# Nine transposed-sum matmuls in one run, sixteen placing loads split over two queues, and a longer wait for host positions

## The chip, the core and the metric

The kernel runs on one core of a Trainium2 chip. The metric is the device time of one execution in microseconds (us). Matrix products run on TensorE (PE), element-wise work on VectorE (DVE) and ScalarE (ACT), and GpSimd (POOL) and SyncE (SP) mainly issue DMA loads and stores; each engine works off its own queue in order.

## The reference

Both halves start from the same normalised input `xn = layernorm(x)`, with 2048 tokens and 576 channels. The result is `x + s * silu(mlp(xn))`.

```
xn = _layernorm(x, axis=-1)
P  = exp((A * dt[:, None])[:, :, None] * pos)
K  = 2.0 * einsum("dn,dnl->dl", C, P).real
y  = irfft(rfft(xn.T, 2L) * rfft(K, 2L))[:L]
s  = y + xn * D_skip
h  = gelu(einsum("bsd,df->bsf", layernorm(xn), w1) + b1)
g  = silu(einsum("bsf,fd->bsd", h, w2) + b2)
out = x + s * g
```

So there is an MLP with 4608 hidden units, and beside it a long convolution per channel whose 2048 taps K come from 128 complex exponentials.

## The kernel before, in words

**The MLP sets the frame.** Hidden units are handled in groups of 384 (three tiles of 128), tokens in blocks of 512. One pair of group and block is a *slot*; there are 48, numbered from 0. A slot has 11 positions: three tiles of layer 1 (line L546, 14 matmuls of 512 columns each, since every fp32 operand is split into a high and a low part), and then eight pieces of layer 2. ACT makes the hidden tile (gelu, L578, then its high part hh, L581) and DVE the low part hl (L584).

Layer 2 in most slots (44 of 48) has two kinds of matmul. *Plain* ones (L638) hold 128 tokens of the hidden tile and stream 448 columns of w2; a key from 0 to 3 names which 128 tokens of the block. The other 128 output channels are computed *turned* (T, L630): w2 is held, 512 tokens are streamed, and the sum lands transposed in a PSUM bank that stays in use over many slots. A slot has nine turned matmuls. The table PLAN (L1296) gives the order of the pieces: a pair like `("T", both)` means the turned matmuls of hidden tiles 0 and 1 (six), `(0, both)` the plain ones of key 0 for the same two tiles (six).

**Four times the turned sums are brought back**, at slots 18, 22, 44 and 45 (CONV). DVE adds the bias (`total_rest`, L651) and transposes 32 by 32 blocks into the tile `bias2` (`turn_rest`, L655). `place_rest` (L657) then moves the blocks to their places in the accumulator with 16 loads from SBUF to SBUF, all from the SP queue (L663).

**The convolution rides between.** Its matmul groups stand as *guests* between pieces of a slot: K is the making of taps from tables (`kgen`, L981, 36 of them), F the first transform (L1053), S the second with the product (L1092), I the inverse (L1145), O the last stage (L1177). A K group may stand alone, or *ride*: go directly in front of another guest, its host (`ride`, L992). The tables for K come from DVE and ACT work on parameters that `load_par` (L876) loads on the POOL queue (L881): a phase product (L899, L902), rounding on ACT (L905), and so on. Chunk results go to DRAM by eight stores on the POOL queue (L1188: four from tile pr, four from tile ys).

**The order of all this is planned while the program is written**, by a small model of the engines (class `Order`): each step has an engine, a duration, a due time, and what it needs. The model's verdict is the order on every engine. `pe_turns` (L1538) lets guests in after certain positions; a K that could stand alone is held back until it has been ready for ALONE us. Loads that are issued inside another step's function, and steps with no engine (such as `load_par`, 4.5 us), take no queue time in the model.

Of the kernel before, what the change touches and what calls it, by code (L numbers as in the profile page):

```python
# [18 lines left out]
P = 128  # L19
# [16 lines left out]
G = 3  # L36
# [3 lines left out]
DA = 448  # L40
# [3 lines left out]
def dve(n):  # L44
    return 0.075 + 0.00104 * n
# [163 lines left out]
def step(eng, dur, fn, need=(), mark=None, cv=0, at=0.0, late=0.0, tbl=None, by=1e9):  # L209
    return dict(eng=eng, dur=dur, fn=fn, need=tuple(need), mark=mark, cv=cv, at=at, late=late, tbl=tbl, by=by)  # L210
# [3 lines left out]
def mixer_kernel(ctx, tc, u, log_a_real, a_imag, c_real, c_imag, log_dt, d_skip, w1, b1, w2, b2,  # L214
                 f1, f2, g2, g1, tvals, ident, out, parts=("mlp", "s4d")):
    nc = tc.nc
# [17 lines left out]
    def dram(ap_of, offset, ap):  # L234
        return bass.AP(tensor=ap_of.tensor, offset=ap_of.offset + offset, ap=ap)
# [30 lines left out]
    bias2 = sb.tile([P, D], F32, name="bias2")  # L266
# [387 lines left out]

        nc.vector.transpose(bias2[:, :TB].rearrange("p (j d) -> p j d", j=4), rest(tb))  # L655

    def place_rest(tb):  # L657

        o = rest(tb)
        x = bias2[:, :TB].rearrange("p (j v d) -> p j v d", j=4, v=4)  # L660
        for c in range(4):
            for v in range(4):
                nc.sync.dma_start(o[32 * v:32 * v + 32, :, 32 * c:32 * c + 32], x[32 * c:32 * c + 32, :, v])  # L663
        if tb == 1:
            nc.sync.dma_start(bias2[:, :DA], dram(b2, 0, [[0, P], [1, DA]]))

    def tanh_half(z):
        t = sb.tile([P, TB], F32, name="h32", bufs=2)[:, :288]
# [541 lines left out]
    NPOS = G + 8  # L1210
    NSLOT = 4 * NG
    od = Order(tc, nc)
# [80 lines left out]
    MA, MT = 0.2034, 0.2303  # L1293
    CONV = {2 * NG - 6: 0, 2 * NG - 2: 1, 4 * NG - 4: 0, 4 * NG - 3: 1}
    both, allof = (0, 1), (0, 1, 2)
    PLAN = [("T", both), (0, both), ("T", (2,)), (0, (2,)), (1, allof), (2, allof), (3, (0,)), (3, (1, 2))]  # L1296
    ENDS = {True: {2: 0, 3: 1, 5: 2, 7: 3}, False: {3: 0, 4: 1, 5: 2, 7: 3}}

    def lens(slot):
# [134 lines left out]
    def weigh_in(which):  # L1434

        m = KB + 1 if which == 1 else G
        ln = lens(turn[0] - 1)
        end = od.t["PE"] + sum(ln[G:] if which == 1 else ln[:G])
        apart = which == 2 and SEQ[turn[0]][0] not in JOINED
        for i in range(m):  # L1440
            by = end - ((2.2, 1.5, 0.4)[i] if apart else 0.8 * (m - i))
            cell = []
            n = (DA, G * DT, 2 * DA)[i] if apart else G * P if which == 1 else D
            k = len(WM)
            WM.append(which)
            wl["steps"].append(step("ACT", act(n), lambda c=cell: c.append(split_raw()), need=[("raw", k + (apart and i == 1))],
                                    mark=("wh", k), by=by - 0.9, at=od.t["PE"] + od.LAT))

            def low(c=cell, k=k, n=n):
                k0 = state["load"]  # L1450
                c[0]()
                for j in range(k0, state["load"]):
                    od.marks["raw", j] = od.t["DVE"] + dve(n) + 5.5 + 1.0 * (j - k0)
            wl2["steps"].append(step("DVE", dve(n), low, need=[("wh", k)], mark=("w", k), by=by))

    WM = [1] * (KB + 1)
# [35 lines left out]
    part = {}  # L1492
# [40 lines left out]

    pace = dict(left=NCH * (2 + 2 + 4), last=0.0, started=False)
    END = 930.0
    ALONE = 5.0

    def pe_turns(limit=1, any_time=False, all_lines=True):  # L1538
        for x in (nl, pl, ml) + ((c3, c1, kl) if all_lines else ()):
            n = 0  # L1540
            while n < (2 if x in (c1, nl) else limit):
                h = od.head(x)
                if h is None or h[0]["eng"] != "PE" or h[1] > od.t["PE"] + (0.3 if x is nl else -0.40):
                    break
                if x is c1:
                    now = od.t["PE"]
                    gap = (END - now) / max(pace["left"], 1)
                    if n == 0 and pace["started"] and now < pace["last"] + 0.50 * gap and not any_time:
                        break
                    pace["started"], pace["last"] = True, now  # L1550
                    pace["left"] -= 1
                if x is kl and pace["started"] and kl["steps"][0]["mark"][1] < NB - 1 and od.t["PE"] < h[1] + ALONE:
                    break
                behind = ride(h[0]) if x in (c1, c3) else None
                od.run(x)
                if behind:
                    behind()
                od.pin()
                od.advance(od.t["PE"])
                n += 1  # L1560
# [64 lines left out]
    for slot in range(NSLOT):  # L1625
        turn[0] = slot + 1
        n, g, tb = SEQ[slot]
        change = slot + 1 < NSLOT and SEQ[slot + 1][0] != n
        final = slot >= NSLOT - 2
        for pos in range(NPOS):  # L1630
# [28 lines left out]
            else:  # L1659
                turned = slot in TURNED  # L1660
                if turned:
                    j, terms, last, hid = l2_terms(pos - G)
# [18 lines left out]
                if j == "T" and slot in CONV and 2 in terms:  # L1681
                    od.urgent.append((od.t["PE"], [step("DVE", dve(TB), lambda tb=tb: total_rest(tb), by=od.t["PE"] + 4.0),
                                                   step("DVE", dve(TB), lambda tb=tb: turn_rest(tb), by=od.t["PE"] + 6.0),
                                                   step("SP", 1.0, lambda tb=tb: place_rest(tb), mark=("placed", slot))]))
                look_ahead(pos)
                if last or halves:
                    add = cell[0]
# [26 lines left out]
            for f in LATER.get((slot, pos), ()):  # L1714
                f()
            od.advance(od.t["PE"])
            pe_turns(all_lines=pos in (0, 1, G + 1, G + 3, G + 5, NPOS - 1))
    od.force(lambda: not od.urgent and not any(x["steps"] for x in od.lines))


# [52 lines left out]
```

## Time and profile before

| | |
|---|---|
| median of 3 runs | 1066.8 us (1066.37 to 1067.03) |
| the profiled execution's own time | 1067.6 us |
| its span, first to last instruction | 1065.4 us |
| granted TensorE clock, mean | 0.999 |
| PE busy | 1057.2 us (99%) |
| DVE busy | 937.1 us (88%) |
| ACT busy | 678.3 us (64%) |
| POOL busy | 212.2 us (20%) |

The span is what the trace covers; the execution's own time is 2.2 us longer, and the profiled execution lies 0.8 us above the median. In rows of the timeline the first number is the start, the second the length from the first start to the last end of the merged instructions. Matmuls overlap: the next starts before the one before has ended, so the time of a matmul is read from start to start, not from its length.

### The profile page before, as it was taken

The numbers are of one execution on the slowest core, as the hardware profiler recorded it, in microseconds if no ns is written. First come the engines' busy times: TensorE is split into PE (matmuls) and PEld (weight loads), VectorE is DVE, ScalarE is ACT, GpSimd is POOL, SyncE is SP. The second block draws the span as 40 slices with busy tenths as digits, with TensorE's granted clock in tenths as the row PEclk, the third lists the DMA queues.
The fourth block names the chain that finished last, engine by engine and source line by source line (L and its number), as shares of the span: only waits on it lengthen the run. The fifth ranks groups of instructions, "written<-read, shape, count | busy, mean of one in ns | idle before, by whom it ended". The sixth has DMA issues, their size and how long they took to land.

```text
span 1065.4 us, 23535 instructions
## 1 busy us (share of the span) xinstructions
PE 1057.2 (99%) x9515; PEld 873.8 (82%) x9515; DVE 937.1 (88%) x1550; ACT 678.3 (64%) x1056; POOL 212.2 (20%) x294
## 2 busy tenths in 40 slices
PE   9999999999999999999999999999999999999997
PEld 7888888888878887888877888788877888778887
DVE  7688768889999899999999999899999999967766
ACT  6658639877655767657666675666685675625344
POOL 5668643201000002000120000200002022322020
PEclk9999999999999999999999999999999999999999
DMA  7785446664223143455521315222422436465146
GB/s 229 238 263 180 124 132 227 220 160 138 64 68 93 43 99 99 120 134 120 122 83 48 110 40 121 70 80 64 97 82 50 132 102 168 123 191 150 29 122 184
DMA packets 149213, 130.93 MB, mean 123 GB/s; under 512 B 99020, under 2 KB 121072, under 8 KB 148080
## 3 DMA queue, kind: packets, MB, share of 16 engines
q1 hardware_dynamic: 132592, 79.76, 28.2%
q0 software_dynamic: 15760, 48.70, 14.8%
q8 instruction: 75, 1.23, 0.5%
q10 hardware_dynamic: 752, 0.97, 0.3%
q14 instruction: 34, 0.28, 0.1%
HBM read 98.90 MB, written 35.19 MB: 126 GB/s over the span
## 4 chain that ended last, share of the span: by engine, by line
PE 89%; DVE 6%; issue 2%; ACT 1%; DMA 1%; ACTq 0%; POOL 0%; DVEq 0%; POOLq 0%
PE m L546 40%; PE m L638 27%; PE m L630 8%; PE cv L981 3%; PE m L608 3%; PE cv L1092 3%; PE cv L1053 2%; PE cv L1145 1%; PE cv L1177 1%; DVE acc L643 1%; PE m L561 1%; DMA acc<-in_A_u_dram 1%; DVE pr L1113 0%; PE cv L608 0%; DVE hl L584 0%
## 5 line engine op out<-in xcount | busy, mean ns | idle before, releaser
L638 PE MATMUL m<-w2s,hh 128*128 128x448 f32 x1056 | 301.6, 367 | 0.4 <-DVE acc L643 0.2
L578 ACT ACTIVATE h<-m,b1t 128x512 f32<-128x512 f32 x144 | 99.3, 690 | 190.0 <-PE m L546 187.6
L638 PEld LDWEIGHTS m<-w2s,hh 128*128 128x128 f32 x1056 | 195.9, 188 | 29.3 <-issue 7.0
L638 PE MATMUL m<-w2s,hl 128*128 128x448 f32 x528 | 191.4, 363 | 0.0
L546 PE MATMUL m<-XH,w1h 128*128 128x512 f32 x564 | 155.5, 397 | 0.0
L546 PE MATMUL m<-XL,w1h 128*128 128x512 f32 x564 | 151.6, 390 | 0.0
L546 PE MATMUL m<-XH,w1l 128*128 128x512 f32 x564 | 151.0, 389 | 0.0
L584 DVE TENSOR_TENSOR hl<-h,hh 128x512 fp32r<-128x512 f32 x144 | 98.7, 686 | 53.6 <-ACT hh L581 53.2
L546 PEld LDWEIGHTS m<-XH,w1h 128*128 128x128 f32 x564 | 103.3, 188 | 30.9 <-issue 9.5
L546 PEld LDWEIGHTS m<-XL,w1h 128*128 128x128 f32 x564 | 105.8, 188 | 23.1
L546 PEld LDWEIGHTS m<-XH,w1l 128*128 128x128 f32 x564 | 105.9, 188 | 22.5
L881 POOL DMA_DIRECT2D par<-par_s x36 | 27.5, 764 | 484.2 <-DVE mg L924 423.6
L643 DVE TENSOR_TENSOR acc<-m,acc 128x448 f32<-128x448 f32 x160 | 98.4, 615 | 19.5 <-PE m L638 18.1
L638 PEld LDWEIGHTS m<-w2s,hl 128*128 128x128 f32 x528 | 99.0, 188 | 7.5
L630 PE MATMUL m<-hh,w2s 128*128 128x512 f32 x264 | 98.8, 401 | 0.0
L581 ACT ACTIVATE hh<-h 128x512 fp32r<-128x512 f32 x144 | 90.7, 631 | 3.3
L530 ACT ACTIVATE w2s<-raw 128x576 fp32r<-128x576 f32 (+3 forms) x75 | 46.4, 676 | 47.6 <-PE m L638 46.7
L924 DVE TENSOR_TENSOR mg<-par 128x1024 f32<-128x1024 f32 x72 | 67.9, 952 | 0.7
L630 PEld LDWEIGHTS m<-hh,w2s 128*128 128x128 f32 x264 | 49.5, 188 | 17.7 <-issue 5.1
L527 DVE TENSOR_TENSOR w1l<-raw,w1h 128x384 fp32r<-128x384 f32 x98 | 49.7, 557 | 13.9 <-ACT w1h L530 13.7
L546 PE MATMUL m<-XR,w1r 128*128 128x512 f32 x141 | 54.8, 389 | 0.0
L546 PE MATMUL m<-XR,w1s 128*128 128x512 f32 x141 | 54.8, 389 | 0.0
(227 smaller groups left out, 1866.1 us busy)
## 6 DMA issues: line engine op xcount, KB each, us to landing
raw<-in_B_w_dram SPq DMA_DIRECT2D x75, 288.0 KB, 3.7
raw<-in_B_w_dram SPq DMA_DIRECT2D x100, 192.0 KB, 3.4
par_s<-A POOLq DMA_DIRECT2D x8, 1080.0 KB, 6.1
par<-par_s POOLq DMA_DIRECT2D x36, 240.0 KB, 3.4
f2t<-f2q SPq DMA_DIRECT2D x24, 256.0 KB, 3.7
raw<-in_B_w_dram SPq DMA_DIRECT2D x50, 96.0 KB, 3.9
u_s<-in_A_u_dram POOLq DMA_DIRECT2D x16, 288.0 KB, 4.2
xc<-xn_s SPq DMA_DIRECT2D x48, 96.0 KB, 4.2
```

Source lines behind the costliest of these rows:

```text
L527: low_on.tensor_sub(lo, r[:m], h[:m].bitcast(F32))
L530: nc.scalar.activation(h, r, AF.Copy)
L546: nc.tensor.matmul(q, a, b, start=j == 0, stop=j == len(ops) - 1)
L578: nc.scalar.activation(t, q, AF.Gelu_apprx_tanh, bias=b1t[:, g * G + i:g * G + i + 1], scale=1.0)
L581: LAST[0] = nc.scalar.activation(hh[:, i], t, AF.Copy)
L584: nc.vector.tensor_sub(hl[:, i], t, hh[:, i].bitcast(F32))
L608: nc.tensor.matmul(q[:, :288], a[:, i, j * P:j * P + P], b[:, i, dh * 288:dh * 288 + 288], skip_group_check=alone, start=i == 0 and k == 0 ...
L630: nc.tensor.matmul(q, a[:, i], b[:, i], start=first and i == 0 and k == 0, stop=slot in CONV and i == G - 1 and k == 2, skip_group_check=True)
L638: nc.tensor.matmul(q[:, :DA], a[:, i, key * P:key * P + P], b[:, i], start=i == 0 and k == 0, stop=i == G - 1 and k == 2)
L643: nc.vector.tensor_add(o, Q2.pop(key)[:, :DA], bias2[:, :DA] if first else o)
L924: nc.vector.tensor_mul(T["m"][:, :, 64 * k:64 * k + 8 * n].rearrange("p c (i j) -> p c i j", i=n), bc(PAR[b][:, :, e8:e8 + n], 3, 8), bc(P ...
L981: nc.tensor.matmul(q[32 * g:32 * g + 32, i // 2, i % 2 * 64:i % 2 * 64 + 64], U[:, ri, 4 * g + i, :], v[:, ri, 4 * g + i, :], start=ri == ...
```

## The change

Five things change in the text of the program. PLAN puts key 0's six plain matmuls of tiles 0 and 1 first and then the nine turned ones without a break. `place_rest` gets a part: eight loads go to the SP queue as before, eight to the POOL queue, and with them the reload of `bias2`. The planner's durations for these follow (5.2 us for each part instead of 1.0 us for all), and the expected landing of raw weights now looks at the SP queue too. ALONE becomes 7 instead of 5. And the position after which guests may come in moves from behind key 0's first six (G + 1) to behind the nine turned ones (G + 2). Since the planner runs anew, rows move on PE in every slot, and on the other engines from about slot 11 on; the first 340 or so instructions of DVE stand as before.

```
--- before.py
+++ after.py
@@ -654,15 +654,16 @@
 
         nc.vector.transpose(bias2[:, :TB].rearrange("p (j d) -> p j d", j=4), rest(tb))
 
-    def place_rest(tb):
+    def place_rest(tb, part):
 
         o = rest(tb)
         x = bias2[:, :TB].rearrange("p (j v d) -> p j v d", j=4, v=4)
-        for c in range(4):
+        queue = (nc.sync, nc.gpsimd)[part]
+        for c in range(2 * part, 2 * part + 2):
             for v in range(4):
-                nc.sync.dma_start(o[32 * v:32 * v + 32, :, 32 * c:32 * c + 32], x[32 * c:32 * c + 32, :, v])
-        if tb == 1:
-            nc.sync.dma_start(bias2[:, :DA], dram(b2, 0, [[0, P], [1, DA]]))
+                queue.dma_start(o[32 * v:32 * v + 32, :, 32 * c:32 * c + 32], x[32 * c:32 * c + 32, :, v])
+        if tb == part == 1:
+            queue.dma_start(bias2[:, :DA], dram(b2, 0, [[0, P], [1, DA]]))
 
     def tanh_half(z):
         t = sb.tile([P, TB], F32, name="h32", bufs=2)[:, :288]
@@ -1293,7 +1294,7 @@
     MA, MT = 0.2034, 0.2303
     CONV = {2 * NG - 6: 0, 2 * NG - 2: 1, 4 * NG - 4: 0, 4 * NG - 3: 1}
     both, allof = (0, 1), (0, 1, 2)
-    PLAN = [("T", both), (0, both), ("T", (2,)), (0, (2,)), (1, allof), (2, allof), (3, (0,)), (3, (1, 2))]
+    PLAN = [(0, both), ("T", both), ("T", (2,)), (0, (2,)), (1, allof), (2, allof), (3, (0,)), (3, (1, 2))]
     ENDS = {True: {2: 0, 3: 1, 5: 2, 7: 3}, False: {3: 0, 4: 1, 5: 2, 7: 3}}
 
     def lens(slot):
@@ -1450,7 +1451,7 @@
                 k0 = state["load"]
                 c[0]()
                 for j in range(k0, state["load"]):
-                    od.marks["raw", j] = od.t["DVE"] + dve(n) + 5.5 + 1.0 * (j - k0)
+                    od.marks["raw", j] = max(od.t["DVE"] + dve(n), od.t["SP"]) + 5.5 + 1.0 * (j - k0)
             wl2["steps"].append(step("DVE", dve(n), low, need=[("wh", k)], mark=("w", k), by=by))
 
     WM = [1] * (KB + 1)
@@ -1533,7 +1534,7 @@
 
     pace = dict(left=NCH * (2 + 2 + 4), last=0.0, started=False)
     END = 930.0
-    ALONE = 5.0
+    ALONE = 7.0
 
     def pe_turns(limit=1, any_time=False, all_lines=True):
         for x in (nl, pl, ml) + ((c3, c1, kl) if all_lines else ()):
@@ -1681,7 +1682,8 @@
                 if j == "T" and slot in CONV and 2 in terms:
                     od.urgent.append((od.t["PE"], [step("DVE", dve(TB), lambda tb=tb: total_rest(tb), by=od.t["PE"] + 4.0),
                                                    step("DVE", dve(TB), lambda tb=tb: turn_rest(tb), by=od.t["PE"] + 6.0),
-                                                   step("SP", 1.0, lambda tb=tb: place_rest(tb), mark=("placed", slot))]))
+                                                   step("SP", 5.2, lambda tb=tb: place_rest(tb, 0)),
+                                                   step("POOL", 5.2, lambda tb=tb: place_rest(tb, 1), mark=("placed", slot))]))
                 look_ahead(pos)
                 if last or halves:
                     add = cell[0]
@@ -1714,7 +1716,7 @@
             for f in LATER.get((slot, pos), ()):
                 f()
             od.advance(od.t["PE"])
-            pe_turns(all_lines=pos in (0, 1, G + 1, G + 3, G + 5, NPOS - 1))
+            pe_turns(all_lines=pos in (0, 1, G + 2, G + 3, G + 5, NPOS - 1))
     od.force(lambda: not od.urgent and not any(x["steps"] for x in od.lines))
```

**PE, second half of slot 18.** The m names are PSUM banks; m_324 and m_341 are the bank of the turned sums, m_3961 and m_3952 key 0, m_4013 and m_3979 key 1. Before:

```order
L638 MATMUL m_3961<-w2s,hh 128x448 x2
L638 MATMUL m_3961<-w2s,hl 128x448
L630 MATMUL m_324<-hh,w2s 128x512
L630 MATMUL m_324<-hl,w2s 128x512
L630 MATMUL m_324<-hh,w2s 128x512
L638 MATMUL m_3961<-w2s,hh 128x448 x2
L638 MATMUL m_3961<-w2s,hl 128x448
L981 MATMUL cv<-v,U 32x64 x32
L638 MATMUL m_4013<-w2s,hh 128x448 x2
```

Now:

```order
L638 MATMUL m_3952<-w2s,hh 128x448 x2
L638 MATMUL m_3952<-w2s,hl 128x448
L630 MATMUL m_341<-hh,w2s 128x512
L630 MATMUL m_341<-hl,w2s 128x512
L630 MATMUL m_341<-hh,w2s 128x512 x2
L630 MATMUL m_341<-hl,w2s 128x512
L630 MATMUL m_341<-hh,w2s 128x512 x2
L630 MATMUL m_341<-hl,w2s 128x512
L630 MATMUL m_341<-hh,w2s 128x512
L638 MATMUL m_3952<-w2s,hh 128x448 x2
L638 MATMUL m_3952<-w2s,hl 128x448
L638 MATMUL m_3979<-w2s,hh 128x448 x2
```

The six plain matmuls (the last of them are the first two rows here) are followed by all nine turned ones; the K group (L981) that stood alone behind key 0 has gone from this place. It now stands further down, directly ahead of the O group, where two rows of the new order read `L982 MATMUL cv<-v,U 32x64 x32` and `L1178 MATMUL cv<-A_83,g1t 32x384 x16`. Over the whole program 14 K groups stood alone and 11 do now; all other groups keep their number.

**POOL, in and after slot 18.** pr and ys are the tiles whose chunk results are stored, par the parameters of the next tables. Before:

```order
L310 DMA u_s<-in_A_u_dram 64x2x576
L881 DMA par<-par_s 128x4x120 x5
L1188 DMA s_s<-pr 32x8x96 x4
L1188 DMA s_s<-ys 32x8x96 x4
L881 DMA par<-par_s 128x4x120 x3
L684 DMA g_s<-acc 128x576 x4
```

Now:

```order
L310 DMA u_s<-in_A_u_dram 64x2x576
L882 DMA par<-par_s 128x4x120 x5
L1189 DMA s_s<-pr 32x8x96 x4
L664 DMA acc<-bias_78 32x4x32 x8
L1189 DMA s_s<-ys 32x8x96 x4
L882 DMA par<-par_s 128x4x120 x3
L685 DMA g_s<-acc 128x576 x4
```

Eight placing loads (L664) stand between the stores from pr and those from ys, and so ahead of the three par loads. The first of these three is the 14th par load of the program in both orders.

**DVE, slot 18 to slot 19.** The names h_ are hidden tiles; L899 (now L900) is the phase product of the 14th tables and reads the 14th par load. Before:

```order
L924 TENSOR_TENSOR mg<-par 128x16x32
L1040 STREAM_TRANSPOSE A_83<-cv 128x12x16x2 x3
L584 TENSOR_TENSOR hl<-h_4125,hh 128x512
L1040 STREAM_TRANSPOSE A_83<-cv 128x12x16x2
L899 TENSOR_TENSOR w<-par,tv 128x1024
L902 TENSOR_TENSOR w<-w,par 128x16x32
L584 TENSOR_TENSOR hl<-h_4192,hh 128x512
L908 TENSOR_TENSOR w<-w 128x1024
L1040 STREAM_TRANSPOSE A_83<-cv 128x12x16x2
L584 TENSOR_TENSOR hl<-h_4218,hh 128x512
```

Now:

```order
L925 TENSOR_TENSOR mg<-par 128x16x64
L1041 STREAM_TRANSPOSE A_83<-cv 128x12x16x2 x4
L584 TENSOR_TENSOR hl<-h_4122,hh 128x512
L900 TENSOR_TENSOR w<-par,tv 128x1024
L903 TENSOR_TENSOR w<-w,par 128x16x32
L584 TENSOR_TENSOR hl<-h_4158,hh 128x512
L925 TENSOR_TENSOR mg<-par 128x16x32
L909 TENSOR_TENSOR w<-w 128x1024
L527 TENSOR_TENSOR w1l<-raw,w1h 128x384
L584 TENSOR_TENSOR hl<-h_4183,hh 128x512
```

The product that reads the 14th par load still stands ahead of the low part of slot 19's second hidden tile (h_4192 before, h_4158 now), with L902 (now L903) between them; the third tile's (h_4218, now h_4183) has one w1l subtraction (L527) more ahead of it. On ACT the rounding that reads L902's result (L905, now L906) stands ahead of the third tile's gelu in both orders.

## Rows read from the trace of the kernel before

**Rows 1.** The page's head and section 1: busy time of PE.

```profile
span 1065.4 us, 23535 instructions
...
PE 1057.2 (99%) x9515; PEld 873.8 (82%) x9515; DVE 937.1 (88%) x1550; ACT 678.3 (64%) x1056; POOL 212.2 (20%) x294
```

**Rows 2.** Timeline of PE, slot 18, from the last turned matmuls on (start, length).

```profile
392.49 0.40 PE L630 MATMUL m<-hh,w2s 128*128 128x512 f32 x1
...
393.18 0.57 PE L638 MATMUL m<-w2s,hh 128*128 128x448 f32 x2
393.59 0.37 PE L638 MATMUL m<-w2s,hl 128*128 128x448 f32 x1
393.88 1.10 PE L981 MATMUL cv<-v,U 128*32 128x64 f32 x64
...
394.92 0.68 PE L638 MATMUL m<-w2s,hh 128*128 128x448 f32 x2
```

**Rows 3.** Timeline of PE, slot 19: a K that rides ahead of an F.

```profile
405.16 0.39 PE L546 MATMUL m<-XR,w1s 128*128 128x512 f32 x1
...
407.34 1.19 PE L546 MATMUL m<-XH,w1h 128*128 128x512 f32 x4
```

**Rows 4.** Timeline of PE, slot 19: an F alone, and the start of layer 2.

```profile
413.59 0.39 PE L546 MATMUL m<-XR,w1s 128*128 128x512 f32 x1
...
414.74 0.50 PE L630 MATMUL m<-hh,w2s 128*128 128x512 f32 x1
415.08 0.40 PE L630 MATMUL m<-hl,w2s 128*128 128x512 f32 x1
```

**Rows 5.** Timeline of PE: the widest wait for a PSUM bank.

```profile
882.67 0.36 PE L638 MATMUL m<-w2s,hl 128*128 128x448 f32 x1
883.22 0.67 PE L638 MATMUL m<-w2s,hh 128*128 128x448 f32 x2 [0.20 <-DVE acc L643]
```

**Rows 6.** Timelines of SP, DVE and POOL around the placing loads of slot 18.

```profile
395.46 11.01 SPq L663 DMA_DIRECT2D acc<-bias  x16
...
394.73 0.70 DVE L655 STREAM_TRANSPOSE bias<-acc 128x512 f32<-128x512 f32 x1
...
403.84 2.31 POOL L1188 DMA_DIRECT2D s_s<-ys  x4
406.14 1.51 POOL L881 DMA_DIRECT2D par<-par_s  x2
```

**Rows 7.** Timeline of POOL: small loads in a row, and one instruction drawn out.

```profile
41.58 6.56 POOL L1344 DMA_DIRECT2D A<-y_s  x12
...
88.52 2.29 POOL L414 TENSOR_SCALAR w<-w,U 128x576 f32<-128x576 f32 x1 [2.06 <-ACT A L855]
...
91.77 8.80 POOL L414 TENSOR_SCALAR w<-w,U 128x576 f32<-128x576 f32 x1
```

**Rows 8.** Timeline of DVE and ACT, slot 19: the product that reads par, and what follows.

```profile
410.60 1.23 DVE L899 TENSOR_TENSOR w<-par,tv 128x1024 f32<-128x1024 f32 x1 [0.54 <-DMA par<-par_s]
411.86 0.69 DVE L902 TENSOR_TENSOR w<-w,par 128x512 f32<-128x512 f32 x1
412.47 0.68 DVE L584 TENSOR_TENSOR hl<-h,hh 128x512 fp32r<-128x512 f32 x1
...
412.59 1.06 ACT L905 ACTIVATE w<-w 128x1024 int32<-128x1024 f32 x1 [0.38 <-DVE w L902]
...
414.02 0.69 ACT L578 ACTIVATE h<-m,b1t 128x512 f32<-128x512 f32 x1 [0.37 <-PE m L546]
...
415.67 0.69 DVE L584 TENSOR_TENSOR hl<-h,hh 128x512 fp32r<-128x512 f32 x1
```

**Rows 9.** Timelines of SP and DVE at the end of the program.

```profile
1033.43 2.71 SPq L732 DMA_DIRECT2D w<-s_s  x6
...
1041.08 0.75 DVE L763 TENSOR_TENSOR w<-w,acc 128x576 f32<-128x576 f32 x1
...
1051.97 0.69 DVE L584 TENSOR_TENSOR hl<-h,hh 128x512 fp32r<-128x512 f32 x1 [1.23 <-ACT hh L581]
```

More of the change, by code (lines that the diff above doesn't have):

```diff
@@ L655, in turn_rest, with place_rest @@
         nc.vector.transpose(bias2[:, :TB].rearrange("p (j d) -> p j d", j=4), rest(tb))
-    def place_rest(tb):
+    def place_rest(tb, part):
         o = rest(tb)
         x = bias2[:, :TB].rearrange("p (j v d) -> p j v d", j=4, v=4)
-        for c in range(4):
+        queue = (nc.sync, nc.gpsimd)[part]
+        for c in range(2 * part, 2 * part + 2):
             for v in range(4):
-                nc.sync.dma_start(o[32 * v:32 * v + 32, :, 32 * c:32 * c + 32], x[32 * c:32 * c + 32, :, v])
-        if tb == 1:
-            nc.sync.dma_start(bias2[:, :DA], dram(b2, 0, [[0, P], [1, DA]]))
+                queue.dma_start(o[32 * v:32 * v + 32, :, 32 * c:32 * c + 32], x[32 * c:32 * c + 32, :, v])
+        if tb == part == 1:
+            queue.dma_start(bias2[:, :DA], dram(b2, 0, [[0, P], [1, DA]]))
     def tanh_half(z):
@@ L1295, in mixer_kernel @@
     both, allof = (0, 1), (0, 1, 2)
-    PLAN = [("T", both), (0, both), ("T", (2,)), (0, (2,)), (1, allof), (2, allof), (3, (0,)), (3, (1, 2))]
+    PLAN = [(0, both), ("T", both), ("T", (2,)), (0, (2,)), (1, allof), (2, allof), (3, (0,)), (3, (1, 2))]
     ENDS = {True: {2: 0, 3: 1, 5: 2, 7: 3}, False: {3: 0, 4: 1, 5: 2, 7: 3}}
@@ L1452, in low @@
                 for j in range(k0, state["load"]):
-                    od.marks["raw", j] = od.t["DVE"] + dve(n) + 5.5 + 1.0 * (j - k0)
+                    od.marks["raw", j] = max(od.t["DVE"] + dve(n), od.t["SP"]) + 5.5 + 1.0 * (j - k0)
             wl2["steps"].append(step("DVE", dve(n), low, need=[("wh", k)], mark=("w", k), by=by))
@@ L1535, in mixer_kernel @@
     END = 930.0
-    ALONE = 5.0
+    ALONE = 7.0
     def pe_turns(limit=1, any_time=False, all_lines=True):
@@ L1683, in mixer_kernel @@
                                                    step("DVE", dve(TB), lambda tb=tb: turn_rest(tb), by=od.t["PE"] + 6.0),
-                                                   step("SP", 1.0, lambda tb=tb: place_rest(tb), mark=("placed", slot))]))
+                                                   step("SP", 5.2, lambda tb=tb: place_rest(tb, 0)),
+                                                   step("POOL", 5.2, lambda tb=tb: place_rest(tb, 1), mark=("placed", slot))]))
                 look_ahead(pos)
@@ L1716, in mixer_kernel @@
             od.advance(od.t["PE"])
-            pe_turns(all_lines=pos in (0, 1, G + 1, G + 3, G + 5, NPOS - 1))
+            pe_turns(all_lines=pos in (0, 1, G + 2, G + 3, G + 5, NPOS - 1))
     od.force(lambda: not od.urgent and not any(x["steps"] for x in od.lines))
```

## The prediction

> **What bounds the kernel now.** I read the page first, then the timeline of PE slot by slot from start to start, then the timelines of the engines that PE waits for. TensorE is busy for 1057.2 us of a span of 1065.4 us [rows 1], and the rest is mostly warm-up and the tail, so the time changes in two ways only: the stream of matmuls itself gets shorter or longer, or something new makes PE wait. The stream is tight. Three turned matmuls take 393.18 - 392.49 = 0.69 us, or 0.23 each, two plain ones 393.59 - 393.18 = 0.41, or 0.20 each [rows 2]. Waits inside the stream are rare; the widest one for a PSUM bank is 883.22 - 882.67 = 0.55 us from start to start where 0.20 is usual, so 0.35 lost [rows 5]. I find four stretched gaps of this kind, at most 4 x 0.35 = 1.4 us together, two of them before slot 11, where the order of DVE stays as it was. DVE, however, waits in one place that matters here: the product L899 in slot 19 starts when its par load lands [rows 8].
>
> **Nine turned matmuls together.** The count of matmuls is the same. What could be saved is the switch between the two kinds, and the rows show hardly any: the turned matmul at a switch takes 0.23 us and the plain pair behind it 0.41, which is 2 x 0.20 within the 0.01 that the rows resolve [rows 2]. At most one such 0.01 in each of 44 slots gives 0 to -0.4 us; I take -0.2. What the first matmuls of layer 2 need is early enough: key 0 needs the same two hidden tiles as the turned six did, at the same moment.
>
> **Guests.** Three K groups fewer stand alone. A K alone stretches the gap between its neighbours to 394.92 - 393.59 = 1.33 us, 1.13 over the usual 0.20 [rows 2]; an F alone to 414.74 - 413.59 = 1.15, 0.92 over the usual 0.23 [rows 4]; K riding ahead of F to 407.34 - 405.16 = 2.18, 1.95 over 0.23 [rows 3]. Riding saves 1.13 + 0.92 - 1.95 = 0.10, and the slow first matmul behind a guest (415.08 - 414.74 = 0.34 instead of 0.23) [rows 4] is paid once instead of twice: 0.11 more. Three times 0.21 is -0.6 us. The move of the guest position from G + 1 to G + 2 puts them behind the turned nine and changes no count.
>
> **Half of the placing loads leave SP.** Sixteen issues hold SP for 11.01 us [rows 6]; half of that is 5.5 us, four times in the program. No row shows PE, DVE or ACT waiting for what stands behind them on SP, so this gain is worth 0. The price of a load on POOL is not shown for this very shape (32 partitions, 4 pieces of 32). The nearest rows: twelve loads of 32 x 4 x 128 in 6.56 us, 0.55 each [rows 7], and four stores of 32 x 8 x 96 in 2.31 us, 0.58 each [rows 6]. I take 0.55, so eight take 4.4 us.
>
> **What the eight loads are put in front of.** This is the step that decides. In the new order of POOL they stand between the stores from pr and those from ys, and behind these comes the 14th par load. The planner doesn't see it, since a par load is a step without an engine. Before, that load is issued at 406.14 [rows 6], and L899 starts at 410.60, after 0.54 us of waiting for it [rows 8]: 4.46 us from issue to use. The eight blocks are ready long before (the transpose L655 starts at 394.73 and takes 0.70 [rows 6]), so they add their own 4.4 us and no more: issue at 410.5, use at 410.5 + 4.46 = 415.0 us.
>
> DVE takes its instructions in order. L899 (now L900) is followed by L902 and by the low part of the second hidden tile, which before ends at 412.47 + 0.68 = 413.15, 2.55 us after L899's start [rows 8]. Now it ends at 415.0 + 2.55 = 417.55. PE wants it in the third plain matmul of tile 1 of key 0. Layer 2 of slot 19 starts at 414.74 [rows 4], less 0.2 for the K that has begun to ride in slot 18, so 414.55; plus 0.11 for the slow first matmul and 5 x 0.20, 415.65. **First wait: 1.9 us.**
>
> The second is behind it. On ACT the rounding L905 waits for L902 and the third tile's gelu stands behind L905. L905 ends at 412.59 + 1.06 = 413.65, 3.05 us after L899's start [rows 8], so now at 418.05, and from the gelu's start to the end of the low part it is (415.67 + 0.69) - 414.02 = 2.34 us [rows 8]: 420.4. PE, already late, wants this low part after the one late matmul, six turned ones and one more: 417.55 + 0.20 + 7 x 0.23 = 419.35. **Second wait: 1.0 us.** DVE is then some 3 us late with the rest of its row, and the addition that frees key 0's bank may be late too: between 0 and 1.8 us (five of the widest waits of rows 5); I take 0.4, one such wait. Together 1.9 + 1.0 + 0.4 = **+3.3 us**. Bounds: 2.3 if the par load lands 1 us sooner, 4.7 with 1.8 in place of 0.4.
>
> At the other three placings no par load that is due soon stands behind. **Tail.** The last O group comes one layer-1 tile later, 14 x 0.23 = 3.2 us. The loads of its result on SP start at 1033.43 now, and DVE uses the first at 1041.08; DVE idles 1.23 us before the last low part [rows 9], so some of it is absorbed: 0 to +0.3, taken as +0.1.
>
> **Sum.** -0.2 - 0.6 + 3.3 + 0.1 = +2.6 us, against the profiled execution's 1067.6 us, which gives 1070.2. That execution lies 0.8 above the median of the runs, so for the median 1066.8 + 2.6 = **1069.4 us**. 0.2% of the median, about what a measurement of this kernel can tell from no change, is 2.1 us: the bounds are 1064.7 and 1068.9.
>
> **A rule that speaks against the change.** POOL instructions can be drawn out: the same L414 takes 2.29 us once and 8.80 another time [rows 7], 3.8 times as long, while the twelve loads in a row kept 0.55 each. The Trainium skill (SBUF — State Buffer, section "SBUF: two separate sides") says that while VectorE runs an instruction in a two-port mode, GpSimd cannot write the descriptors of loads issued from its queue; by its example in the next section, 620 ns alone and about 3100 ns beside such an instruction, the eight would take an estimated 8 x 3.1 = 25 us, 20 more than by the rows, and the sum would be near 1090 us. The trace's loads on POOL show no such length, so the sum keeps 0.55.
>
> **The rivals.**
> - *The wait is short; not slower.* The par load lands sooner after its issue than 4.46 us. The first wait is gone from 1.9 us sooner on (a landing after 2.55 us), and with 2 us sooner what is left is the second wait, at most 1 us. The other terms are -0.2 - 0.6 + 0.1 = -0.7, so the time is 1066.8 - 0.7 + 1.0 = 1067.1 us. For it: DVE's wait before was only 0.54 us, so the load's landing is known from that place alone. Against it: the chain L900, L903, L906 and gelu is in order on both engines, with nothing to overtake.
> - *Waits for banks besides.* DVE is retimed from slot 11 on, and every slot has a bank wait in reach. Seven more of the widest (7 x 0.35 = 2.5 us) on top give 1069.4 + 2.5 = 1071.9 us. Against it: the planner keeps due times for exactly these additions, and only two such waits stand after slot 11 now.
> - *Drawn-out issues on POOL.* If each of the eight is stretched as L414 was, they take 8 x 0.55 x 3.8 = 16.7 instead of 4.4 us, the par load is 12.3 us later, and PE waits that much more: 1069.4 + 12.3 = 1081.7 us. Against it: none of the twelve loads of rows 7 was drawn out. The rule of the Trainium skill above is of this kind, and its example is longer still.
> - *The change does no more than it says,* all of its savings at their ends and no new wait: -0.4 - 0.6 - 0.7 (the two bank waits after slot 11) = 1065.1 us at best; to pass 1064.7 it would need still more from the reordered guests.
>
> **How the numbers follow.** The forecast has 0.58; its bounds reach from 1066.8 - 0.7 + 2.3 = 1068.4 to 1066.8 - 0.7 + 4.7 = 1070.8 us, and I put 0.48 of it over 1068.9 and 0.10 under. The short wait has 0.23, all within 0.2%; bank waits besides 0.09 and drawn-out issues 0.02, both slower; the savings alone 0.08, of which 0.06 would count as faster, since guests that move may also meet fewer waits of their own. So faster 0.06, same 0.23 + 0.10 + 0.02 = 0.35, slower 0.48 + 0.09 + 0.02 = 0.59. The range from 1066.2 to 1071.9 us leaves out the savings alone, drawn-out issues, the upper half of the bank waits and the lowest short waits, about 0.17.
>
> **What would show it.** In the new trace, eight L664 rows on POOL between the stores from pr and from ys near 404 us, some 4.4 us long; L900 on DVE with an idle time of about 5 us that ends with the par load; then in slot 19 an L638 row of PE that waits some 2 us for DVE's hl, and an L630 row that waits about 1 us more. Wrong would be: L900 that starts before 413.0 us, POOL issues far from 0.55 us, PE gaps of over 0.3 us in many other slots, or a PE that passes slot 19 without a wait while the time still moves by more than 1 us.

## The result and the profile after

The change made the kernel slower: a median of 1071.35 us (1070.54 to 1071.85, five runs) beside 1066.8 us before (1066.21 to 1067.1, five runs). The ratio is 1.0043, with an interval of 1.0028 to 1.0058. The forecast was 1069.4 us, and the range 1066.2 to 1071.9 us holds the time. The direction was right, and the size was too small: +4.55 us instead of +2.6.

The profiled execution took 1071.01 us. The head of its page and its busy times, which answer to [rows 1]:

```profile
span 1069.2 us, 23544 instructions
...
PE 1058.5 (99%) x9515; PEld 874.5 (82%) x9515; DVE 936.8 (88%) x1550; ACT 683.0 (64%) x1061; POOL 228.4 (21%) x328
```

The busy times of PE and DVE hardly moved, and the span grew by 3.8 us. So PE waited. The view of waits for PE says for what (engine, line, what it waited for; in total, times, longest):

```profile
PE m L638 <- DVE hl L584: 1.8, 1, 1.8
PE m L1241 <- POOL XL L1232: 1.3, 1, 1.3
...
PE m L638 <- DVE acc L643: 0.6, 1, 0.6
```

The second row is the start of the program, the same in both kernels. The first and the third stand in one slot, number 19. Here are its first matmul and that of slot 20, from the timeline of PE before and after:

```profile
402.19 1.09 PE L546 MATMUL m<-XH,w1h 128*128 128x512 f32 x4
425.17 1.09 PE L546 MATMUL m<-XH,w1h 128*128 128x512 f32 x4
```

```profile
401.42 1.09 PE L546 MATMUL m<-XH,w1h 128*128 128x512 f32 x4
428.90 1.09 PE L546 MATMUL m<-XH,w1h 128*128 128x512 f32 x4
```

Slot 19 took 22.98 us before and takes 27.48 now: +4.50 us, as much as the whole change of the median. Behind it PE loses nothing more: from slot 20 to the last matmul it gains 0.49 us on before. (The span grew by less than slot 19 did because this execution also reaches slot 19 0.77 us sooner. That is no gain of the change: e4 below, with before's order on PE, starts slot 19 at 401.35.)

POOL in this stretch (start, length; rows of several issues are joined), which answers to [rows 6]:

```profile
401.09 2.33 POOL L1189 DMA_DIRECT2D s_s<-pr  x4 [16.64 <-ACT pr L1186]
403.42 4.38 POOL L664 DMA_DIRECT2D acc<-bias  x8
407.79 2.32 POOL L1189 DMA_DIRECT2D s_s<-ys  x4
411.31 0.77 POOL L882 DMA_DIRECT2D par<-par_s  x1 [1.19 <-issue]
```

The eight placing loads take 4.38 us, 0.55 each. The par load behind them is issued at 411.31 instead of 406.14; 1.19 us of that is a gap for which the profile names no cause. DVE in slot 19, for [rows 8]:

```profile
414.48 1.22 DVE L900 TENSOR_TENSOR w<-par,tv 128x1024 f32<-128x1024 f32 x1 [6.03 <-DMA par<-par_s]
...
416.34 0.68 DVE L584 TENSOR_TENSOR hl<-h,hh 128x512 fp32r<-128x512 f32 x1
...
419.16 0.69 DVE L584 TENSOR_TENSOR hl<-h,hh 128x512 fp32r<-128x512 f32 x1
```

And PE, layer 2 of slot 19:

```profile
414.71 0.56 PE L638 MATMUL m<-w2s,hh 128*128 128x448 f32 x2
417.08 0.54 PE L638 MATMUL m<-w2s,hl 128*128 128x448 f32 x1 [1.81 <-DVE hl L584]
...
421.03 0.57 PE L638 MATMUL m<-w2s,hh 128*128 128x448 f32 x2
...
423.24 0.36 PE L638 MATMUL m<-w2s,hl 128*128 128x448 f32 x1
424.16 0.68 PE L638 MATMUL m<-w2s,hh 128*128 128x448 f32 x2 [0.56 <-DVE acc L643]
```

Three losses can be read here. The matmul at 417.08 starts 2.37 us after the pair ahead of it, where 2 x 0.20 is usual: 1.97 us. From 417.08 to 421.03 there are one plain and nine turned matmuls, 3.95 us where 0.20 + 9 x 0.23 = 2.27 is usual: 1.68 us. Then 424.16 - 423.24 = 0.92 where 0.20 is usual, and 0.11 in the slow first matmul behind it: 0.83 us. Together 4.48.

The middle one has its explanation in the stretches of 2 us (stretch; length, PE busy, matmuls, granted clock, DMA share, GB/s):

```profile
414.00:416.00 2.00, 1.27 (x13) 1.00 0.03 8
416.00:418.00 2.00, 0.92 (x3) 0.84 0.00 0
418.00:420.00 2.00, 2.00 (x7) 0.50 0.27 67
420.00:422.00 2.00, 2.00 (x9) 0.81 0.42 123
422.00:424.00 2.00, 1.60 (x9) 1.00 0.93 298
```

After PE had stood still, the granted clock fell to 0.50, the lower level of 1.2 GHz, and came back to 1.00 near 421 us. The prediction had no such term.

### The profile page after: what moved, and what is told of

The parts are those of the page before. It is cut to its first block, busy times and chain, and to the rows that moved or that the text cites. A ratio compares the mean times of both kernels' runs of the same rounds, so it can differ in the third digit from the quotient of the medians.

```text
span 1069.2 us, 23544 instructions
## 1 busy us (share of the span) xinstructions
PE 1058.5 (99%) x9515; PEld 874.5 (82%) x9515; DVE 936.8 (88%) x1550; ACT 683.0 (64%) x1061; POOL 228.4 (21%) x328
## 4 chain that ended last, share of the span: by engine, by line
PE 95%; DVE 2%; DMA 1%; POOL 1%; issue 1%; ACT 0%; SPq 0%; ACTq 0%; DVEq 0%; POOLq 0%
PE m L546 42%; PE m L638 30%; PE m L630 8%; PE cv L1093 3%; PE cv L982 3%; PE m L608 3%; PE cv L1054 2%; PE cv L1146 2%; PE cv L1178 1%; PE m L561 1%; DMA acc<-in_A_u_dram 0%; PE cv L608 0%; POOL s_s L1189 0%; POOL acc L664 0%; DMA row<-y_s 0%
## 5 line engine op out<-in xcount | busy, mean ns | idle before, releaser
L630 PE MATMUL m<-hh,w2s 128*128 128x512 f32 x264 | 90.2, 396 | 0.0
L530 ACT ACTIVATE w2s<-raw 128x576 fp32r<-128x576 f32 (+3 forms) x75 | 46.3, 675 | 36.9 <-PE m L638 35.3
L527 DVE TENSOR_TENSOR w1l<-raw,w1h 128x384 fp32r<-128x384 f32 x98 | 49.8, 555 | 9.7 <-ACT w1h L530 9.6
L906 ACT ACTIVATE w<-w 128x1024 int32<-128x1024 f32 x36 | 37.9, 1054 | 28.8 <-DVE w L903 28.6
```

The source lines that it names most:

```text
L527: low_on.tensor_sub(lo, r[:m], h[:m].bitcast(F32))
L530: nc.scalar.activation(h, r, AF.Copy)
L630: nc.tensor.matmul(q, a[:, i], b[:, i], start=first and i == 0 and k == 0, stop=slot in CONV and i == G - 1 and k == 2, skip_group_check=True)
L906: nc.scalar.activation(T["w"][:, 0].bitcast(I32), T["w"][:, 1], AF.Copy)
```

## The experiments

The theory (A): the eight loads hold up the 14th par load, DVE is late by that, and all of slot 19's loss follows. The rivals: the new order on DVE and PE is at fault; POOL issues cost by themselves; the low clock is a cost of its own.

| run | what it is | median us | ratio to before, interval | slot 19, us |
|---|---|---|---|---|
| e1 | the change, sixteen loads on SP | 1066.55 | 1.0002 (0.9994 to 1.0011) | 23.29 |
| e2 | the change, four on POOL | 1068.61 | 1.0019 (1.001 to 1.0029) | 24.29 |
| (the change) | eight on POOL | 1071.35 | 1.0043 (1.0028 to 1.0058) | 27.48 |
| e12 | the change, ten on POOL | 1071.2 | 1.0042 (1.0025 to 1.0059) | 27.83 |
| e3 | the change, twelve on POOL | 1073.56 | 1.0072 (1.0058 to 1.0085) | 30.07 |
| e5 | the change, eight on POOL ahead of pr | 1067.44 | 1.0001 (0.9992 to 1.001) | 24.34 |
| e6 | the change, PE kept at work | 1070.47 | 1.0039 (1.0027 to 1.0052) | 27.54 |
| e10 | the change, old patience | 1071.53 | 1.005 (1.0037 to 1.0064) | 27.52 |
| e4 | before, split alone | 1066.59 | 1.0006 (0.9998 to 1.0015) | 22.98 |
| e7 | before, PLAN alone | 1066.94 | 0.9999 (0.9991 to 1.0008) | 23.02 |
| e8 | before, patience alone | 1078.09 | 1.0112 (1.0097 to 1.0128) | 23.02 |
| e9 | before, patience and split | 1070.73 | 1.0042 (1.0029 to 1.0054) | 24.48 |
| e11 | before, PLAN, patience, split of e4 | 1070.99 | 1.0042 (1.003 to 1.0055) | 24.42 |

**How many of the loads stand on POOL (e1, e2, e3).** The orders on PE, DVE and ACT stay those of the change.

```
-        queue = (nc.sync, nc.gpsimd)[part]
+        queue = nc.sync                              # e1
-        for c in range(2 * part, 2 * part + 2):
+        for c in ((0, 1, 2), (3,))[part]:            # e2
+        for c in ((0,), (1, 2, 3))[part]:            # e3
```

> The changed kernel with all sixteen placing loads on SP; the planner and the order on PE, DVE and ACT stay as they are. Theory A (the eight loads on POOL hold up the 14th par load, and everything lost in slot 19 follows from that): slot 19 is 4.5 us shorter, the wait of 1.97 us for hl, the matmuls at the lower clock and the wait for the bank all go together, and the time is 1071.35 - 4.5 = 1066.9 us. Rival B (the loss is that of the new order on DVE and PE, and the par load is only the last thing that is seen): DVE's idle time before L900 shrinks, but PE still waits, and the time stays over 1070 us.

> Four placing loads on POOL instead of eight, twelve on SP. Theory A: the par load is issued 4 x 0.55 = 2.2 us sooner, L900 starts near 412.3 us, the second low part is there 0.2 us before PE wants it; the first wait is gone, of the second up to 0.7 us is left, and TensorE keeps its full clock. Time 1066.9 to 1068.4 us, 1067.5 taken. A rival in which the loss falls evenly with the number of loads: half of 4.5 us is left, 1069.1 us. Rival B: over 1070 us.

> Twelve placing loads on POOL, four on SP. Theory A: the par load is 2.2 us later, PE waits 1.97 + 2.2 = 4.2 us for the same hl, and what follows (eight slow matmuls, the bank) costs what it cost with eight loads: 1071.35 + 2.2 = 1073.6 us. If the lower clock lasts longer after a longer wait, up to 1 us more. Rival B: no change from 1071.35 us.

With all on SP the loss is gone (1066.55 us, 1066.9 expected): slot 19 is down to 23.29 us, and the one wait left in it is of 0.18 us from start to start, for a bank. (The profiled execution of e1, 1068.73 us, was its slowest, with waits of PE near 467, 517 and 528 us that are shorter or absent in the other runs with this order.) With twelve the time grew by 2.2 us (1073.56, 1073.6 expected). So the order alone is not at fault.

With four, 1068.61 us was over the 1066.9 to 1068.4 expected. Slot 19 explains only part: it is 1.00 us longer than in e1. In the profiled execution of e2 PE also lost 0.93 us near 82 us, long before the first placing load, so that part is not the loads' doing. What slot 19 shows is that PE waits there for no low part, but for a bank (timeline of PE in e2):

```profile
422.22 0.68 PE L638 MATMUL m<-w2s,hh 128*128 128x448 f32 x2 [1.00 <-DVE acc L643]
```

L900 of e1, e2 and e3, one row from the timeline of DVE of each:

```profile
410.51 1.22 DVE L900 TENSOR_TENSOR w<-par,tv 128x1024 f32<-128x1024 f32 x1 [1.78 <-DMA par<-par_s]
```

```profile
412.53 1.23 DVE L900 TENSOR_TENSOR w<-par,tv 128x1024 f32<-128x1024 f32 x1 [2.77 <-DMA par<-par_s]
```

```profile
417.45 1.23 DVE L900 TENSOR_TENSOR w<-par,tv 128x1024 f32<-128x1024 f32 x1 [8.58 <-DMA par<-par_s]
```

Slot 19 starts in these runs at 401.66, 402.69 and 401.82, and slot 20 at 424.95, 426.98 and 431.89. From L900's start to the slot's end it is 14.44, 14.45 and 14.44 us; in the changed kernel 428.90 - 414.48 = 14.42. With this order on DVE, PE loses what L900 is late, microsecond for microsecond, whatever the waits are that it shows. From L900 on DVE works without an idle time over 0.15 us up to the addition that frees the bank for the next key (the first and last rows of that stretch are shown under e6), and PE can't be past that bank sooner. In e1 the addition starts 9.06 us after L900 and in the changed kernel 9.05; from the wait's end to the end of the slot it is 4.75 and 4.74 us.

**Is the low clock a price of its own (e6)?** Ten matmuls were put in front of layer 2 of slot 19; they repeat the first matmul of key 0, which overwrites them, so the output stays what it was.

```
+        for _ in range(10 if slot == 19 and key == 0 and terms[0] == 0 else 0):
+            nc.tensor.matmul(q[:, :DA], hh[:, 0, key * P:key * P + P], h[:, 0], start=True, stop=True)
         for i in terms:
```

> The changed kernel with ten more matmuls at the start of layer 2 of slot 19: the first matmul of key 0 is repeated, and overwritten by the real one, 10 x 0.20 = 2.0 us, so that TensorE works through the time in which it waited 1.97 us for hl. Theory A1 (the low clock cost 1.7 us of its own): the clock stays up, the 1.7 us go, and the time is 1071.35 - 1.7 = 1069.7 us or up to 0.7 us more. Theory A2 (DVE works without a pause from L900 to the addition that frees key 1's bank, so PE gets that bank at the same moment whatever its clock was): the clock stays up, the waits for the third low part and for the bank grow by what is won, and the time stays at 1071.35 us.

1070.47 us, 1.0039 beside 1.0043: nothing that can be told, and with intervals of this width the time alone can't decide between a gain of 1.7 us and none. The trace does. Slot 19 takes 27.54 us beside 27.48, although the clock stayed up, stretch by stretch (columns as above):

```profile
414.00:416.00 2.00, 2.00 (x18) 1.00 0.04 8
416.00:418.00 2.00, 2.00 (x11) 1.00 0.00 0
418.00:420.00 2.00, 1.55 (x6) 1.00 0.26 37
420.00:422.00 2.00, 1.99 (x10) 1.00 0.45 127
422.00:424.00 2.00, 1.16 (x6) 1.00 0.93 300
```

What the faster matmuls won went into two waits (PE; the line numbers of layer 2 are higher by two here):

```profile
418.66 1.03 PE L630 MATMUL m<-hh,w2s 128*128 128x512 f32 x2
420.01 0.50 PE L630 MATMUL m<-hl,w2s 128*128 128x512 f32 x1 [0.33 <-DVE hl L584]
...
422.79 0.37 PE L640 MATMUL m<-w2s,hl 128*128 128x448 f32 x1
424.28 0.67 PE L640 MATMUL m<-w2s,hh 128*128 128x448 f32 x2 [1.12 <-DVE acc L645]
```

From start to start that is 420.01 - 418.66 - 2 x 0.23 = 0.89 us for the third low part and 424.28 - 422.79 - 0.20 = 1.29 for the bank. The bank comes at 424.28, 22.79 us after the slot's start, and it came at 424.16, 22.74 us after it, with the low clock. The row of DVE that sets it, from L900 (here L902) to the addition:

```profile
414.58 1.23 DVE L902 TENSOR_TENSOR w<-par,tv 128x1024 f32<-128x1024 f32 x1 [6.02 <-DMA par<-par_s]
...
422.22 1.50 DVE L1043 STREAM_TRANSPOSE A<-cv 128x384 f32<-128x384 f32 x3
423.65 0.58 DVE L645 TENSOR_TENSOR acc<-m,acc 128x448 f32<-128x448 f32 x1
```

No row between these shows idle time. So the low clock lay beside DVE's work and cost nothing here.

**Is it the queue or the place in it (e4, e5)?** In e4 before's `place_rest` takes `(nc.sync, nc.gpsimd)[c // 2]`, with the planner untouched. In e5 the change's two steps write all out at the first of them (indentation left out):

```
-step("SP", 5.2, lambda tb=tb: place_rest(tb, 0)),
-step("POOL", 5.2, lambda tb=tb: place_rest(tb, 1), mark=("placed", slot))
+step("SP", 5.2, lambda tb=tb: [place_rest(tb, k) for k in both]),
+step("POOL", 5.2, lambda: None, mark=("placed", slot))
```

> The kernel before with nothing changed but the queue of eight placing loads (POOL in place of SP); its PE, DVE and ACT orders are those of before. Theory A: the par load is issued 4.4 us later, up to 1.2 us more for the gap that POOL showed ahead of it, L899 starts at 413.7 to 414.9 us instead of 410.60, and PE waits in slot 19 for the low parts, 2 to 4 us with what follows: 1069 to 1071 us, 1069.8 taken. Rival B (the new order is at fault, not the queue): 1066.8 us as before.

> The changed kernel with the eight POOL loads written out together with the eight of SP, so that on POOL they stand ahead of the stores from pr instead of behind them; still eight on SP and eight on POOL, and the order on every other engine stays. Theory A, narrowed by the run with the split alone (the queue costs nothing where POOL only waits for pr; what costs is to stand behind pr and ahead of the par load): the eight take 4.4 us of the 16.6 us in which POOL waits for pr, the par load is issued near 406 us, slot 19 loses nothing, and the time is that with all sixteen on SP, 1066.5 us. Rival (eight loads on POOL cost by themselves, by the 1.2 us gap or by what they move on the DMA engines): over 1068 us.

e4 refuted what was expected of it: 1066.59 us, no loss that can be told, and slot 19 as long as before. Its POOL rows show why, and e5's are alike:

```profile
394.89 4.35 POOL L663 DMA_DIRECT2D acc<-bias  x8 [10.74 <-DVE bias L655]
400.67 2.31 POOL L1188 DMA_DIRECT2D s_s<-pr  x4 [1.43 <-ACT pr L1185]
402.97 2.31 POOL L1188 DMA_DIRECT2D s_s<-ys  x4
406.28 1.52 POOL L881 DMA_DIRECT2D par<-par_s  x2 [1.00 <-DVE mg L924]
```

Written out at once, the eight fall into the time in which POOL waits for pr anyway. In the change the planner's step for POOL stands behind 5.2 us of a step for SP, so the loads are written out later, behind the stores from pr, and there they are in the way of the par load. The same eight loads on the same queue cost 4.5 us in slot 19 in one place of it, and in the other nothing (e4) or about 1 us (e5): e5's slot 19 is 24.34 us long, 1.05 more than e1's, because its par load is issued at 407.95 instead of 405.95, behind another gap, of 2.33 us, whose cause isn't known.

**The other parts alone (e7, e8, e10).** e7 is before with the new PLAN line, e8 before with ALONE 7 and G + 2, e10 the change without these two.

> The kernel before with the new PLAN alone: the nine turned matmuls together, guests and placing loads as before (all sixteen on SP). Prediction: 0 to -0.4 us, so 1066.2 us beside 1066.4 for before, no change that can be told. Rival (guests that now split the turned run, or additions with new due times, cost bank waits): 1067 to 1068 us.

> The kernel before with ALONE 7 and the guest position G + 2 alone. Prediction: fewer K groups alone, 0.21 us each, and no new wait: -0.6 us for three groups, 1065.8 us beside 1066.4 for before. Rival (later guests make DVE's work on them late, with bank waits of 0.3 us and the last results later): 1067 to 1069 us.

> The changed kernel with the old patience (ALONE 5, G + 1); nine together, split and the planner's two steps as changed. The eight loads still stand between pr and ys on POOL, ahead of the 14th par load. Theory A: slot 19 loses about 4 us as in the changed kernel: 1066.8 + 4 = 1070.8 us. Rival (the lateness in slot 19 needs the moved guests as well): 1067 us.

Nine together: nothing that can be told. e10 loses in slot 19 as the change does, 27.52 us; the moved guests are not needed for it. (The guests stand elsewhere there, and from L900 to the slot's end it is 13.60 us, so 14.44 belongs to the change's order and isn't a constant of the kernel.) e8 was a surprise: 11 us slower. Its wait is at the end of the program (PE, slot 46, which takes 9.0 us longer than before in the profiled execution, the fastest of the four):

```profile
1032.65 2.97 PE L1177 MATMUL cv<-A,g1t 64*32 64x384 f32 x32 [6.76 <-DVE A L1161]
```

SP, in the same stretch:

```profile
1013.70 10.78 SPq L663 DMA_DIRECT2D acc<-bias  x16
1025.81 0.33 SPq L665 DMA_DIRECT2D bias<-in_B_b_dram  x1
1026.20 0.42 SPq L473 DMA_DIRECT2D raw<-in_B_w_dram  x1
```

A load of weights stands behind sixteen placing loads and a reload that waits for all of them. ACT's rounding of these weights (L530) waits for it, DVE's part (L527) for ACT, the transposes L1161 stand behind that on DVE, and PE's last O group waits for these. In before all three weight loads of this group stood ahead of the sixteen on SP. So the rival of late guests was near, and its mechanism was another: the guests moved, DVE's order with them, and one load fell behind the placings.

The Trainium skill (DMA: Bandwidth & Descriptors, section "Issuing engines are not separate DMA queues") says that spreading issues over engines saves only the sequencer's time for issuing, usually small beside the transfer. In e8 that time is the 10.78 us of the row above, not small, and PE waited 6.8 us behind it.

**What the split and the planner's steps repair (e9, e11).** e9 is e8 with e4's split, e11 is e9 with the new PLAN, so the change without its new steps and marks; in both the reload of `bias2` stays on SP, which the change puts on POOL.

> The kernel with the new patience (ALONE 7, G + 2) and, besides, eight of the placing loads on POOL; the orders of PE, DVE and ACT are those of the run with the patience alone. Theory S (what that run lost at the end, 8.9 us, is a load of weights that stood on SP behind sixteen placing loads of 0.65 us each): with eight ahead of it the load is issued some 5.4 us sooner, its wait of 6.8 us shrinks to 1.4 us or less, the matmuls at the lower clock go with it, and the time is 1078.1 - 8 = 1070 us or less. Rival (the last guests are late by themselves): it stays over 1075 us.

> The kernel before with the new PLAN, the new patience and the split, but without the planner's new steps and marks, so that the eight POOL loads are written out at once and stand ahead of the stores from pr. Theory A: nothing is late in slot 19 and, with the split, nothing at the end: 1066 to 1068 us, 1066.8 taken. Rival (a cost of the patience itself is left): 1069 us or more.

e9, at 1070.73 us just over the 1070 expected, gained 7.4 us on e8, which bears the theory out; eight loads less on SP bring the weights' load from 1026.20 to 1022.55, and the wait of PE from 6.8 to 2.2 us. That is over the 1.4 expected: the load is issued 3.65 us sooner and not 5.4, since the eight take 6.27 us on SP and the reload L665 still waits 1.3 us behind them for all placings. Slot 19, 24.48 us, holds 1.5 us more of e9's loss. e11 missed: 1070.99 us where 1066.8 was expected. PE waits 2.7 us at the same place, and slot 19 is 24.42 us long.

What the new steps and marks repair can be read by comparing e11 with the changed kernel, where PE has no wait at the end. In both the last O group stands behind the second layer-1 tile of slot 46. Two things differ. The load of weights is issued 2.83 us after the slot's start in e11 (1022.86 - 1020.03) and 0.06 us after it in the changed kernel (1022.88 - 1022.82). And on DVE the last two transposes for O stand behind the part of these weights in e11:

```profile
1027.18 0.76 DVE L527 TENSOR_TENSOR w2s<-raw,w2s 128x576 fp32r<-128x576 f32 x1 [4.09 <-ACT w2s L530]
1027.86 1.30 DVE L1161 STREAM_TRANSPOSE A<-A 128x512 f32<-128x512 f32 x2
```

and ahead of it in the changed kernel:

```profile
1025.84 1.29 DVE L1162 STREAM_TRANSPOSE A<-A 128x512 f32<-128x512 f32 x2
...
1028.24 0.75 DVE L527 TENSOR_TENSOR w2s<-raw,w2s 128x576 fp32r<-128x576 f32 x1
```

e1 has the steps and marks, but its reload is on SP: it has the changed kernel's order on DVE, issues the load 0.30 us after the slot's start, and has no wait there. So the reload's queue isn't needed for the repair; how much each of the two differences is worth isn't shown. But the same steps put the eight loads behind pr.

**Ten on POOL (e12),** as a test of two patterns seen so far (the dots stand for the unchanged arguments).

```
-        for c in range(2 * part, 2 * part + 2):
+        for c in range(4):
             for v in range(4):
-                queue.dma_start(...)
+                if (4 * c + v >= 6) == bool(part):
+                    queue.dma_start(...)
```

> Ten placing loads on POOL, six on SP, the rest as in the changed kernel. Two things are asked. The rule of the six runs with this order on DVE: slot 19 ends 14.44 us after L900 starts. The ten take 5.45 us, so the par load is issued at about 412 us, L900 starts between 415.2 and 416.4 us, slot 19 is 28.2 to 29.4 us long and the time about 1072.5 us. The gap of POOL ahead of the par load: in the runs so far it stands behind 3072 pieces counted from the first store of pr (a placing load has 32 x 4 = 128, a store 32 x 8 = 256): by that rule it now stands behind the third store of ys (1024 + 1280 + 768). If it is counted in instructions (16 in the changed kernel), behind the second; if it belongs to the par load itself, directly ahead of that.

```profile
401.01 2.33 POOL L1190 DMA_DIRECT2D s_s<-pr  x4 [16.66 <-ACT pr L1187]
403.33 5.43 POOL L665 DMA_DIRECT2D acc<-bias  x10
408.75 1.74 POOL L1190 DMA_DIRECT2D s_s<-ys  x3
410.90 0.58 POOL L1190 DMA_DIRECT2D s_s<-ys  x1 [0.42 <-issue]
411.48 0.78 POOL L883 DMA_DIRECT2D par<-par_s  x1
```

(Line numbers are higher by one here.) L900 (here L901) starts at 414.72, slot 20 at 429.16: 14.44 us, as forecast. The gap stands behind the third store of ys, as counted in pieces. The size was missed: L900 was expected at 415.2 or later and the time at 1072.5 us, and it is 1071.2, no more than with eight. The gap is only 0.42 us long, and L900 starts 3.24 us after the par load's issue, so it is but 0.33 us later after the slot's start than with eight.

No run beats the kernel before. With the loss in slot 19 down to 0.3 us (e1) or 1.4 us (e5), the change can't be told from it.

## Why the prediction was right in direction and short in size

- **The place and the mechanism were right.** Eight rows of 0.55 us on POOL, the par load behind them, L900 with 6.03 us of idle time, PE waiting for the second low part. L900 started at 414.48; 415.0 was forecast. Two errors partly cancelled there, which is luck: the load was issued 0.8 us later than forecast (the gap of 1.19), and L900 started 3.17 us after that issue instead of 4.46.
- **First wait:** 1.9 forecast, 1.97 measured. L900 was 0.5 us early, and PE was as well: layer 2 of slot 19 began at 413.99 and not at 414.55.
- **Second wait:** 1.0 forecast. With the clock up it is there, 0.89 us in e6. In the changed kernel PE reached the row only after the low part was done (419.16 + 0.69 = 419.85), since it was slow itself: 1.68 us of slow matmuls stand in the wait's place.
- **The addition that frees a bank: this is the term that was mis-sized.** The prediction put 0.4 us, "one such wait", between 0 and 1.8, as if DVE's lateness were mostly used up by then. Measured, it is 0.83 us behind the slow matmuls, and 1.29 behind fast ones. The step that failed is adding up waits of PE one by one. L900 sits 14.44 us ahead of the slot's end, with DVE at work up to the addition and PE behind it, so one number, L900's delay, gives the loss, and the three waits only share it out. The prediction had that number: 415.0 - 410.60 = 4.4 us. Taken whole in place of its 3.3 us it gives +3.7 us, nearer to the measured 4.55. Measured from e1 to the changed kernel, L900 is 4.21 us later after the slot's start, and the slot is 4.19 us longer. That none of the delay is absorbed is shown by e1, where PE already waits for that bank; the rows of before didn't show it.
- **The range:** the forecast's own bounds, 1068.4 to 1070.8 us, don't hold 1071.35. The range holds it only because it reaches up for the rival of bank waits in many slots, which isn't what happened.
- **Savings of -0.8 us** (switches and guests) can't be told in the time: e1, which has all of them and only 0.18 us of waiting in slot 19, is at 1.0002 (0.9994 to 1.0011). The profiled executions show a part. From slot 2 to slot 19 PE takes 350.87 us beside 350.89 before; from slot 20 to the last matmul it takes 0.49 us less (0.3 to 0.7 less in e2, e3, e5 and e12). Short waits of 0.1 to 0.4 us each, from start to start, stand in other places than before, near 87, 329, 472, 858 and 899 us, but hardly in greater number: before they are near 87, 106, 670 and 883.
- **"Worth 0" for SP** was right with before's guests (e4) and wrong with the change's: in e8 a load behind SP's sixteen issues cost most of 11 us. The prediction costed the split and the patience apart, and they only make sense together. The sum wasn't hurt by it, since the changed kernel has both.
- **The tail** was put at +0.1. PE shows no wait there; from the start of the last matmul to the end of the span there are 5.8 us before and 6.4 after, but 5.8 to 6.4 in the runs with the change's own order on PE (e1: 5.8), so nothing can be told.
- **Rivals.** The short wait fell, though its premise came in part: L900 followed the par load's issue 1.3 us sooner than forecast, but that issue was 0.8 us later than forecast. Drawn-out issues didn't come: 4.38 us for eight. The Trainium skill's rule (SBUF — State Buffer, "SBUF: two separate sides"), by which a VectorE instruction in a two-port mode locks GpSimd out of writing descriptors, is not put to the test here: DVE worked beside these issues without a pause, on products, additions and transposes, and an issue kept 0.55 us (0.54 in e4 and e12), but the trace doesn't say whether any of these instructions ran in that mode. Bank waits besides, 1071.9 us, came nearest in time; its waits stand in the one slot, not in many.

## What to carry to other kernels

When a late input makes an in-order engine late, don't add up the waits that it causes. Ask for how long that engine then works without a pause and who needs the last result: the loss is the lateness, less the slack at that one point. A load costs by its place in a queue more than by its queue: the same eight issues were free, or cost 1 us, inside a wait that POOL had anyway, and cost 4.5 us behind it. And a planner that doesn't count a queue's time (par loads on POOL, weights on SP) can put something due behind something long; costing one part of a change without the other can be wrong by more than the whole, as 11 us for the patience alone shows.

## What was unexpected of the hardware

- **A lower clock that cost nothing.** After 1.97 us of standing still PE ran ten matmuls in 3.95 us instead of 2.27, at a granted clock of 0.50 in the middle of them. Keeping it at 1.00 (e6) left slot 19 as long, 27.54 us beside 27.48. Elsewhere it may cost: in e8 slot 46 takes 9.0 us longer than before, for a wait of 6.8, and the granted clock is 0.50 from 1032 to 1036 us; how much of the rest is the clock's wasn't separated.
- **A gap of POOL behind a certain number of pieces.** In the changed kernel, e3, e4, e5, e6, e9, e10, e11 and e12 POOL stands still in slot 19 for 0.4 to 2.5 us, and each time 3072 pieces have been issued since the first of the placing loads and stores (32 x 4 = 128 for a placing load, 32 x 8 = 256 for a store, by their shapes): behind the fourth store of ys with eight loads, the second with twelve, the third with ten. (e10 has 0.18 us more behind the eighth load.) In before, e1, e2, e7 and e8, with fewer pieces ahead of the par load, there is no gap. The profile puts it down to nothing, or to rows of DVE; in e5 it names the transposes L1041, but e1, with the same order, issued that load before they were done. The pattern was forecast for e12 and held; its cause wasn't found, and that the count of pieces is the cause is not shown.
